# A fused attention and gated-MLP kernel: output tiles gated by their loads in the issue-order model, dummy matmuls up to the first scores, and another plan table

## The chip, the cores and the metric

The kernel runs on one core of one Trainium2 chip. The metric is device time in microseconds (us) of one execution; several executions are timed and the median is quoted with the range. Engines: PE is TensorE (PEld its weight loads), ACT is ScalarE, DVE is VectorE, POOL is GpSimd, SP is SyncE, which here only issues transfers (SPq is its queue). Every run of the changed kernel and of the experiments also reports the mean clock that the TensorE throttle granted; for the kernel before of the first rounds only the profiled execution has one.

## The reference

Two branches share one layer norm: an attention with 32 heads of 20 elements over 2,048 rows, and a gated MLP of 1,728 hidden units. The output is the input plus attention times the SiLU of the MLP.

```python
x = A_x                                   # 1 x 2048 x 640, bf16
xn = layernorm(x)
q, k, v = split(xn @ wqkv)                # 32 heads of 20
p = softmax(q @ k.T * 20 ** -0.5)
s = (p @ v) @ wo
h = sigmoid(xn @ w_gate) * (xn @ w_up)    # 2048 x 1728
g = silu(h @ w_down)
return x + s * g
```

## The kernel before

The scores are cut into 2,048 jobs of 128 x 512 (32 blocks, each of four heads and 512 rows). For most jobs ACT takes the exponential from PSUM; for the rest DVE approximates it (`iv`, then three passes `pb`). The three large engines work side by side for some 765 us, and the order in which each gets its instructions is found while the kernel is built: a time-stepped **order model** with fixed durations (`now`, `free[engine]`) hands out the next instruction to each engine. Its weights come from a **plan table** with one row of 18 numbers for each of the 32 blocks. No decision is taken on the chip: the model only fixes orders, and a wrong duration in it shows up as an engine standing at the head of its queue (in the profile of before DVE stands 1.08 us for a load, up to 695.40).

The parts that the change touches, with cuts:

```python
PLAN = (
    (0.25, 5, 0.15, 0.2, 0.5, 0, 0.4, 1, 0.0, 2, 2, 0, 0, 2, 4, 48, 1, 1),
    ...                                     # 32 rows
)
...
def dummies(n):                             # prologue; warm[0] is read by nobody
    for _ in range(n):
        nc.tensor.matmul(warm[0][:, 0:P], lhsT=ident, rhs=ident, start=True, stop=True)

def s_warm(eng):                            # first work of PE, at 2.5 us
    warm.append(psP.tile([P, 512], FP32, tag="pk", bufs=1, name="warm"))
    dummies(54)
...
def s_k(eng, c):                            # the four K matmuls of the first group
    pks[c] = psP.tile([P, 512], FP32, tag="pk", bufs=1, name="psk")
    k_mm(pks[c], 0, c)
def s_bound(eng):                           # the last PE work ahead of the first scores
    q_bound(pq[0], 0, pq[1])
...
def load_out(tt):                           # loads for one tile of 128 output rows
    ...
    nc.sync.dma_start(out=out_tiles[tt][0], in_=x2[tt * P:(tt + 1) * P, :])
    nc.sync.dma_start(out=out_tiles[tt][1], in_=gq_dram[tt * P:(tt + 1) * P, :])

def mk_out(tt, h, at):                      # half an output tile: 5 matmuls, one DVE pass, one addition
    def alloc():
        if h == 0:
            load_out(tt)
            if tt == 0:
                load_out(1)
        ...
    def ev():
        ... nc.vector.scalar_tensor_tensor(out=tmp, in0=st["ps"], scalar=0.25, in1=gqr[:, sl], ...)   # "otmp"
        add = nc.vector if h == 1 and claimed[0] == NJOB * NBLK else nc.gpsimd
        add.tensor_tensor(out=xr[:, sl], in0=tmp, in1=xr[:, sl], op=ALU.add)
        if h == 1:
            nc.sync.dma_start(out=out2[tt * P:(tt + 1) * P, :], in_=xr)
            if tt + 2 < TT - 4 and ...:
                load_out(tt + 2)
...
# end of a block: DVE copies the sums ("on<-bk"), they go to DRAM and come back as 128 x 16 ("lt<-ld")
free["DVE"] = now + T_ON
timed.append((free["DVE"] + 6.5, norm_pending[0]) + norm_a(norm_pending[0]))   # then DVE's reciprocal "rt<-lt"
```

Of the kernel before, what the change touches and what calls it, by code (L numbers as in the profile page):

```python
# [18 lines left out]
P = 128  # L19
# [19 lines left out]
            dmax=2, third=2, dord=0, mord=0, mfew=2, npv=4, held=48, burst=1, excl=1)  # L39
KEYS = tuple(RULE)  # L40
PLAN = (
    (0.25, 5, 0.15, 0.2, 0.5, 0, 0.4, 1, 0.0, 2, 2, 0, 0, 2, 4, 48, 1, 1),
    (0.25, 5, 0.15, 0.2, 0.5, 0, 0.4, 1, 0.0, 2, 1, 0, 3, 2, 4, 48, 1, 1),
    (0.25, 4, 0.15, 0.2, 0.8, 0.2, 0.4, 1, 8.0, 2, 2, 0, 0, 2, 4, 48, 1, 1),
    (0.25, 4, 0.15, 0, 0.8, 0.2, 0.4, 1, 0.0, 2, 2, 0, 0, 2, 4, 48, 0, 1),
    (0.25, 4, 0.15, 0, 0.8, 0.2, 0.4, 1, 0.0, 2, 2, 3, 0, 2, 4, 48, 0, 0),
    (0.2, 4, 0.15, 0.2, 0.2, 0.2, 0.4, 1, 0.0, 2, 2, 0, 0, 1, 4, 32, 1, 1),
    (0.25, 4, 0.15, 0.5, 0.8, 0.2, 0.4, 1, 0.0, 2, 2, 0, 0, 2, 4, 48, 1, 1),
    (0.25, 4, 0.3, 0.2, 0.35, 0.2, 0.4, 1, 0.0, 2, 2, 0, 0, 1, 4, 48, 1, 1),
    (0.25, 4, 0.3, 0.2, 0.35, 0.8, 0.4, 1, 0.0, 2, 2, 0, 0, 1, 4, 48, 1, 1),  # L50
    (0.3, 4, 0.3, 0.2, 0.35, 0.8, 0.4, 1, -2.0, 2, 2, 0, 0, 1, 4, 48, 1, 1),
    (0.3, 4, 0.3, 0.2, 0.35, 0.8, 0.4, 1, -2.0, 2, 2, 0, 0, 1, 4, 48, 1, 1),
    (0.25, 4, 0.15, 0.2, 0.2, 0.2, 0.4, 1, 0.0, 2, 2, 0, 0, 2, 4, 48, 0, 1),
    (0.2, 4, 0.15, 0.2, 0.2, 0.2, 0.2, 1, 0.0, 2, 2, 0, 0, 2, 4, 48, 0, 1),
    (0.25, 4, 0.15, 0.2, 0.2, 0.2, 0.4, 1, 0.0, 2, 0, 0, 0, 1, 4, 48, 0, 1),
    (0.25, 4, 0, 0.2, 0.2, 0.2, 0.4, 1, 0.0, 2, 0, 0, 0, 1, 4, 48, 1, 1),
    (0.25, 4, 0, 0, 0.2, 0.2, 0.4, 1, 4.0, 2, 0, 0, 0, 1, 4, 48, 1, 1),
    (0.3, 4, 0.15, 0.2, 0.2, 0.2, 0.4, 1, 0.0, 2, 2, 0, 0, 2, 4, 48, 1, 1),
    (0.3, 4, 0.15, 0.2, 0.2, 0.5, 0.7, 1, 0.0, 2, 2, 0, 0, 2, 4, 48, 1, 1),
    (0.25, 4, 0.15, 0.2, 0.2, 1.2, 0.4, 1, 0.0, 2, 2, 0, 0, 2, 4, 48, 1, 1),  # L60
    (0.25, 4, 0.15, 0.2, 0, 1.2, 0.4, 1, 0.0, 2, 2, 0, 0, 2, 4, 48, 1, 1),
    (0.25, 4, 0.3, 0.2, 0, 1.2, 0.4, 1, 0.0, 2, 2, 0, 0, 1, 4, 48, 1, 1),
    (0.25, 4, 0.3, 0.2, 0.5, 1.2, 0.4, 1, 0.0, 2, 1, 0, 0, 1, 4, 48, 1, 1),
    (0.25, 4, 0, 0.2, 0.8, 1.2, 0.4, 1, 0.0, 2, 2, 0, 0, 2, 4, 48, 1, 1),
    (0.25, 4, 0.15, 0.2, 0.2, 0.5, 0.4, 1, 0.0, 2, 1, 0, 0, 2, 4, 48, 1, 1),
    (0.45, 4, 0.15, 0.2, 0.2, 0.5, 0.4, 1, 0.0, 2, 1, 2, 0, 2, 4, 52, 1, 1),
    (0.25, 4, 0.15, 0.2, 0.2, 0.2, 0.4, 1, 0.0, 2, 1, 0, 0, 2, 4, 48, 1, 1),
    (0.25, 4, 0.15, 0.2, 0.2, 0.5, 0.4, 1, 0.0, 2, 1, 0, 0, 2, 4, 48, 1, 1),
    (0.25, 4, 0.15, 0.5, 0.2, 1.2, 0.4, 1, 0.0, 2, 2, 0, 2, 2, 4, 48, 1, 1),
    (0.25, 4, 0.15, 0.2, 0.35, 0.2, 0.4, 1, 0.0, 2, 2, 0, 0, 2, 4, 48, 1, 1),  # L70
    (0.25, 4, 0.15, 0.2, 0.2, 0.2, 0.4, 1, 0.0, 2, 0, 0, 0, 2, 4, 48, 1, 1),
    (0.25, 4, 0.15, 0.2, 0.35, 0.8, 0.4, 1, 14.0, 2, 1, 0, 0, 2, 4, 48, 1, 1),
    (0.25, 4, 0.15, 0.2, 0.2, 0.2, 0.4, 1, 0.0, 2, 2, 0, 0, 2, 4, 48, 1, 1),
)

PRO = (
# [35 lines left out]
def kernel(  # L112
# [146 lines left out]
    with tc.tile_pool(name="ln", bufs=2) as lp, \  # L259
# [105 lines left out]
        def s_k(eng, c):  # L365
            pks[c] = psP.tile([P, 512], FP32, tag="pk", bufs=1, name="psk")
            k_mm(pks[c], 0, c)

        def s_km(eng, c):
            maxed.append(c)  # L370
# [29 lines left out]

        def s_bound(eng):
            q_bound(pq[0], 0, pq[1])

        def s_qe0(eng):
            q_evac(pq[0], qts[0])
# [104 lines left out]
    def mk_k(g, c, at):  # L510
        st = {}

        def alloc():
            st["ps"] = misc_ps()
        mms = [lambda kd=kd: k_mm1(st["ps"], g, c, kd) for kd in range(KD)]
        return Item([("PE", alloc, [(T_MM, f) for f in mms]),
                     ("DVE", 0.66, lambda: k_evac(st["ps"], g, c), "free"),
                     ("DVE", 0.60, lambda: k_max(g, c), "", lambda t: mds_done(g, t))], at)

    def mds_done(g, t):  # L520
        if len(mk_n[g]) == NQC:
# [45 lines left out]
    def mk_ku(u, c, at):  # L567
        st = {}

        def alloc():  # L570
            st["ps"] = misc_ps()

        def ev():
            st["k"] = wk.tile([P, QC], BF16, tag="ku", bufs=2, name="ku")[0:UC, :]
            nc.vector.tensor_copy(out=st["k"], in_=st["ps"][0:UC, :])
            nc.sync.dma_start(out=kD[u][:, c * QC:(c + 1) * QC], in_=st["k"])

        def mx():
            if u not in mku:
                mku[u] = [wk.tile([UC, NQC], FP32, tag="mk4", bufs=2, name="mk4"), 0, None]  # L580
            nc.vector.tensor_reduce(out=mku[u][0][:, c:c + 1], in_=st["k"], axis=AXISX, op=ALU.max,
                                    apply_absolute_value=True)
            mku[u][1] += 1
            if mku[u][1] == NQC:
                mk = wk.tile([UC, 1], FP32, tag="mk", bufs=2, name="mk")
                nc.vector.tensor_reduce(out=mk, in_=mku[u][0], axis=AXISX, op=ALU.max)
                mku[u][2] = wk.tile([UC, UH], BF16, tag="mdu", bufs=2, name="mdu")
                nc.vector.tensor_scalar_mul(out=mku[u][2], in0=esum_u[0:UC, :], scalar1=mk[:, 0:1])

        def end(t):  # L590
            if mku[u][1] == NQC:
                ev_at[("mdu", u)] = t + 0.3
        return Item([("PE", alloc, [(T_MM, lambda kd=kd: u_mm(st, u, 1, c, kd)) for kd in range(KD)]),
                     ("DVE", 0.60, ev, "free", mark("kD", u, c)), ("DVE", 0.60, mx, "", end)], at,
                    pre=[("wu", u)])

    aqs = {}
# [180 lines left out]
    def load_out(tt):  # L778
# [3 lines left out]
        out_tiles[tt] = (o2[:, 0:D], o2[:, D:3 * D].bitcast(FP32))  # L782
        nc.sync.dma_start(out=out_tiles[tt][0], in_=x2[tt * P:(tt + 1) * P, :])
        nc.sync.dma_start(out=out_tiles[tt][1], in_=gq_dram[tt * P:(tt + 1) * P, :])

    def pool_hold(t):
        pool_from[0] = max(pool_at[0], t)
# [2 lines left out]
    def mk_out(tt, h, at):  # L790
        st = {}

        def alloc():
            if h == 0:
                load_out(tt)
                if tt == 0:
                    load_out(1)
            st["ps"] = misc_ps()

        def mm(kd):  # L800
# [4 lines left out]
        def ev():  # L805
# [7 lines left out]
            if h == 1:  # L813
                nc.sync.dma_start(out=out2[tt * P:(tt + 1) * P, :], in_=xr)
                if tt + 2 < TT - 4 and all(("d", (tt + 2) // 4, t4, i) in ev_at for t4 in range(4) for i in range(2)):
# [1 line left out]
        return Item([("PE", alloc, [(0.136, lambda kd=kd: mm(kd)) for kd in range(KD)]),  # L817
                     ("DVE", 0.40, ev, "free", lambda t: (mark("o", tt, h)(t), pool_hold(t)))], at, need=blk(NG - 1, tt // 4),
                    pre=[("d", tt // 4, t4, i) for t4 in range(4) for i in range(2)] + [("wo",), ("oc", tt // 4)] + (
                        [("o", tt - 2, 1)] if h == 0 and tt > 1 else []))  # L820


    wdf = wd.rearrange("p k e -> p (k e)")[:, 0:8 * D].bitcast(FP32)
# [290 lines left out]
    with tc.manual_schedule(engines={ENG.PE, ENG.Activation, ENG.DVE}):  # L1114
# [64 lines left out]
        while chain or items or glu_items or o_next < NQC or any(it.i < len(it.ops) for it in active):  # L1179
# [10 lines left out]
            if ("wo",) not in ev_at and base() >= PAIR and ("bD", NU - 1) in ev_at and all(  # L1190
                    v_at.get((NG // 2 - 1, t), 1e9) <= now for t in range(TT)) and all(
                    ev_at.get(("h", 2, kf), 1e9) <= now for kf in range(NFT)):
                ev_at[("wo",)] = now + 6.0
                for kd in range(KD):
                    nc.sync.dma_start(out=wo[kd], in_=A_wo[kd * P:(kd + 1) * P, :])
                for i in range(2):
# [35 lines left out]
            for eng in ("ACT", "DVE"):  # L1232
# [7 lines left out]
                    continue  # L1240
                if eng == "DVE" and norm_pending is not None and norm_pending[1] <= now and norm_pending[0] < NBLK - 1:
                    free["DVE"] = now + T_ON
                    timed.append((free["DVE"] + 6.5, norm_pending[0]) + norm_a(norm_pending[0]))
                    flex[pv_bank[0]] = now + T_ON + EL["DVE"]
                    pv_bank[0] = None
                    norm_pending = None
# [269 lines left out]
```

## Time and profile before

| | before |
|---|---|
| time | 811.13 us, 3 runs, 810.94 to 812.6 |
| profiled execution | span 811.3 us (time 813.0), mean granted clock 0.988 |
| busy share PE / DVE / ACT | 96% / 95% / 97% |
| first exponential to last | 29.88 to 795.51 us |
| from the last exponential to the end | 15.8 us |

The page gives the busy shares, the slices and the chain of waits; its own clock row already shows a dent in the second and in the tenth slice. The lines are in the prediction below, with their reading.

### The profile page before, as it was taken

What the parts mean: (1) busy time and instruction counts of PE and PEld (TensorE: products, weight loads), DVE (VectorE), ACT (ScalarE), POOL (GpSimd) and SP (SyncE); (2) the same over time, 40 slices, a digit from 0 to 9 for tenths busy, and PEclk for the clock granted to TensorE, in tenths of its full rate; (3) what the DMA queues carried; (4) which work ended last, traced back from release to release, by engine and by line L of the source; (5) the groups of instructions that cost most, each with busy time, mean ns of one, the idle gap of its engine ahead of it and who ended that gap; (6) DMA issues with size and microseconds to landing.
All of it is one profiled execution on the core that took longest, in us unless ns stands there. A gap on an engine that the chain in (4) does not pass through costs nothing.

```text
span 811.3 us, 17165 instructions
## 1 busy us (share of the span) xinstructions
PE 774.9 (96%) x6490; PEld 276.9 (34%) x6490; DVE 774.2 (95%) x1272; ACT 783.8 (97%) x1003; POOL 93.2 (11%) x107
## 2 busy tenths in 40 slices
PE   7899999999999999999999999999999999899995
PEld 6422233333333333333323323333332233233332
DVE  8799999998999999999999999999999999999996
ACT  8799999998999999999999999999999999999992
POOL 6000000000000000000000000000000001401346
PEclk9899999998999999999999999999999999999998
DMA  5511311122122222321113323143122331510431
GB/s 165 173 45 48 101 48 50 53 60 75 55 73 60 72 78 66 96 61 50 37 56 85 91 82 83 50 129 90 41 87 68 84 91 29 159 51 26 142 122 56
DMA packets 95876, 62.62 MB, mean 77 GB/s; under 512 B 36388, under 2 KB 89684, under 8 KB 95792
## 3 DMA queue, kind: packets, MB, share of 16 engines
q1 hardware_dynamic: 95504, 61.18, 26.9%
q8 instruction: 51, 0.84, 0.4%
q14 instruction: 33, 0.27, 0.1%
q10 hardware_dynamic: 288, 0.33, 0.1%
HBM read 47.84 MB, written 13.55 MB: 76 GB/s over the span
## 4 chain that ended last, share of the span: by engine, by line
ACT 55%; PE 28%; DVE 10%; issue 4%; DMA 2%; POOL 0%; SPq 0%; DVEq 0%; ACTq 0%; POOLq 0%
ACT pt L142 48%; PE scA L928 9%; PE bk L964 6%; PE bk L742 6%; DVE iv L1305 4%; PE bk L704 3%; ACT tnh L142 3%; DVE pb L1022 1%; PE bk L564 1%; ACT td L142 1%; DVE pb L1016 1%; DVE pb L1019 1%; PE bk L672 1%; ACT sq L338 1%; PE bk L802 1%
## 5 line engine op out<-in xcount | busy, mean ns | idle before, releaser
L142 ACT ACTIVATE pt<-scA 128x1024 bf16<-128x1024 f32 x696 | 715.0, 1235 | 2.7 <-PE bk L928 2.0
L1305 DVE TENSOR_SCALAR iv<-bk 128x512 int16<-128x512 f32 x497 | 330.5, 679 | 12.0 <-PE bk L928 10.5
L928 PE MATMUL scA<-q,kT 32*128 32x512 bf16 x1391 | 272.1, 384 | 15.7 <-ACT pt L142 11.6
L928 PE MATMUL bk<-q,kT 32*128 32x512 bf16 x657 | 206.6, 387 | 0.8 <-DVE otmp L809 0.5
L964 PE MATMUL bk<-pt,v 128*21 128x512 bf16 x1551 | 180.7, 382 | 0.0
L928 PEld LDWEIGHTS <-kT 32*128 32x128 bf16 x2048 | 86.7, 91 | 266.1 <-issue 253.7
L964 PE MATMUL bk<-pb,v 128*21 128x512 bf16 x994 | 155.8, 383 | 0.7 <-DVE pb L1016 0.5
L1022 DVE TENSOR_TENSOR pb<-iv,pb 128x2048 bf16<-128x2048 bf16 (+1 forms) x125 | 151.6, 1212 | 0.4
L704 PE MATMUL bk<-xnT,wgu 128*128 128x512 bf16 x520 | 144.3, 382 | 1.4 <-DVE iv L1305 0.6
L142 ACT ACTIVATE pt<-bk 128x512 bf16<-128x512 f32 x160 | 129.1, 807 | 4.3 <-PE bk L928 2.3
L1001 POOL TENSOR_TENSOR on_bf<-on,rl 128x512 bf16<-128x512 f32 x31 | 42.2, 1363 | 662.9 <-DVE rl L999 576.0
L1016 DVE TENSOR_SCALAR pb<-iv 128x2048 int16<-128x2048 int16 (+1 forms) x125 | 88.4, 707 | 0.7
L742 PE MATMUL bk<-wd,hT 128*128 128x320 bf16 x448 | 87.8, 307 | 1.2 <-DVE hT L724 1.0
L1019 DVE TENSOR_SCALAR pb<-iv 128x2048 int16<-128x2048 int16 (+1 forms) x125 | 85.9, 687 | 0.1
L964 PEld LDWEIGHTS <-v 128*21 128x21 bf16 x2545 | 47.5, 90 | 86.6 <-issue 70.2
L704 PEld LDWEIGHTS <-wgu 128*128 128x128 bf16 x520 | 39.0, 97 | 64.5 <-issue 41.7
L742 PEld LDWEIGHTS <-hT 128*128 128x128 bf16 x448 | 35.8, 98 | 43.9 <-issue 33.1
L142 ACT ACTIVATE tnh<-bk 128x512 bf16<-128x512 f32 (+1 forms) x56 | 45.9, 819 | 0.1
L564 PE MATMUL bk<-xnT,wu 128*128 128x512 bf16 x160 | 44.4, 382 | 0.0
L712 DVE SCALAR_TENSOR_TENSOR hT<-tnh,bk 128x512 bf16<-128x512 bf16 x52 | 35.4, 681 | 1.1 <-PE bk L704 0.5
L812 POOL TENSOR_TENSOR xnT<-otmp,xnT 128x320 bf16<-128x320 f32 x24 | 24.7, 1044 | 42.4 <-DVE otmp L809 30.6
L672 PE MATMUL bk<-wv,xnT 128*128 128x160 bf16 x280 | 28.2, 245 | 0.2
(116 smaller groups left out, 391.8 us busy)
## 6 DMA issues: line engine op xcount, KB each, us to landing
rl<-rd SPq DMA_DIRECT2D x124, 64.0 KB
wgu<-in_B_w_gate_dram SPq DMA_DIRECT2D x24, 320.0 KB
wgu<-in_B_w_up_dram SPq DMA_DIRECT2D x24, 320.0 KB
gq_dram<-gqs SPq DMA_DIRECT2D x24, 160.0 KB
xnT<-gq_dram SPq DMA_DIRECT2D x12, 320.0 KB
xt<-in_A_x_dram SPq DMA_DIRECT2D x16, 160.0 KB
oD<-on_bf SPq DMA_DIRECT2D x120, 20.0 KB
wd<-in_B_w_down_dram SPq DMA_DIRECT2D x1, 2080.0 KB
```

What stands on the lines that cost most here:

```text
L142: return nc.scalar.add_instruction(mybir.InstActivation(func=func, name=nc.get_next_instruction_name(), engine=ENG.Activation, ins=[nc.sca ...
L564: nc.tensor.matmul(st["ps"], lhsT=wus[u][:, kd, i, :], rhs=xnT[:, c, kd, :], start=(kd == 0), stop=(kd == KD - 1))
L672: nc.tensor.matmul(st["ps"][:, i * 2 * GC:(i + 1) * 2 * GC], lhsT=xn_tok(tts[i], kd), rhs=wvs[pr][:, kd, :], start=(kd == 0), stop=(kd == ...
L704: nc.tensor.matmul(st[key][0:fs, :], lhsT=w[:, i, kd, ko * P:ko * P + fs], rhs=xnT[:, c, kd, :], start=(kd == 0), stop=(kd == KD - 1))
L742: nc.tensor.matmul(st["ps"][:, 0:HD], lhsT=hT[0:fsz[kf], kf, t4 * P:(t4 + 1) * P], rhs=wd[0:fsz[kf], kf, h * HD:(h + 1) * HD], start=(kf = ...
L928: nc.tensor.matmul(dst, lhsT=kTs[gc(b)[0] % 2][32 * j:32 * j + 32, kt * P:(kt + 1) * P], rhs=qts[b % 3][32 * j:32 * j + 32, :], start=True ...
L964: nc.tensor.matmul(bank[pv_bank[0]][32 * j:32 * j + DH + 1, :], lhsT=lhsT, rhs=u["src"], start=first, stop=last, tile_position=(0, 32 * j) ...
L1001: nc.gpsimd.tensor_tensor(out=on_bf, in0=on, in1=rl, op=ALU.mult)
L1016: nc.vector.tensor_scalar(out=pb[:, 0, :, :].bitcast(I16), in0=iv, scalar1=0x7F80, scalar2=1, op0=ALU.bitwise_and, op1=ALU.bitwise_or)
L1019: nc.vector.tensor_scalar(out=pb[:, 1, :, :].bitcast(I16), in0=iv, scalar1=0x007F, scalar2=0x3F00, op0=ALU.bitwise_and, op1=ALU.bitwise_or)
L1022: nc.vector.tensor_tensor(out=pb[:, 1, :, :], in0=iv.bitcast(BF16), in1=pb[:, 1, :, :], op=ALU.mult)
L1305: nc.vector.tensor_scalar(out=d["iv"][:, j, :], in0=bank[bk], scalar1=B_OFF, scalar2=0.0, op0=ALU.add, op1=ALU.max)
```

## The change

The intent: (1) let the order model know when the loads of an output tile land, so that DVE is not sent to a tile whose data is not there; (2) keep PE busy before the first scores, so that its clock is not halved there (0.50 from 27.81 to 34.64 us in the profile of before); (3) a plan table found anew (another seed of the search) for the changed model. Two durations are also made truer: DVE's last maximum of a group takes 1.05 instead of 0.60 us, and the reciprocal comes 7.0 instead of 6.5 us after the copy of the sums.

```diff
 PLAN = (
-    (0.25, 5, 0.15, 0.2, 0.5, 0, 0.4, 1, 0.0, 2, 2, 0, 0, 2, 4, 48, 1, 1),
+    (0.25, 4, 0.3, 0.2, 0.2, 0.2, 0.4, 1, 0.0, 2, 0, 0, 2, 2, 4, 48, 1, 1),
 ...                                  all 32 rows
         def s_k(eng, c):
             ...
             k_mm(pks[c], 0, c)
+            if len(pks) == NQC:
+                warm[0] = psP.tile([P, 2 * P], FP32, tag="tp", bufs=4, name="warm2")
+                dummies(14)
 ...
             q_bound(pq[0], 0, pq[1])
+            dummies(10)
 ...
-                     ("DVE", 0.60, lambda: k_max(g, c), "", lambda t: mds_done(g, t))], at)
+                     ("DVE", 1.05 if c == NQC - 1 else 0.60, lambda: k_max(g, c), "", lambda t: mds_done(g, t))], at)
 ...
         nc.sync.dma_start(out=out_tiles[tt][1], in_=gq_dram[tt * P:(tt + 1) * P, :])
+        ev_at[("ol", tt)] = now + 4.0
 ...
                 load_out(tt)
-                if tt == 0:
-                    load_out(1)
 ...
-                        [("o", tt - 2, 1)] if h == 0 and tt > 1 else []))
+                        [("o", tt - 2, 1)] if h == 0 and tt > 1 else []), gates={1: [("ol", tt)]})
 ...
                 ev_at[("wo",)] = now + 6.0
+                load_out(0)
+                load_out(1)
 ...
-                    timed.append((free["DVE"] + 6.5, norm_pending[0]) + norm_a(norm_pending[0]))
+                    timed.append((free["DVE"] + 7.0, norm_pending[0]) + norm_a(norm_pending[0]))
```

## The prediction

> **What bounds the kernel now.** I read the page first (busy shares, slices, the chain that ended last), then the engines' busy times by stretch, then the timeline of the worst stretches, since the page alone says only that everything is full.
>
> ```profile
> span 811.3 us, 17165 instructions
> PE 774.9 (96%) x6490; PEld 276.9 (34%) x6490; DVE 774.2 (95%) x1272; ACT 783.8 (97%) x1003; POOL 93.2 (11%) x107
> ...
> PEclk9899999998999999999999999999999999999998
> ...
> ACT 55%; PE 28%; DVE 10%; issue 4%; DMA 2%; POOL 0%; SPq 0%; DVEq 0%; ACTq 0%; POOLq 0%
> ...
> L142 ACT ACTIVATE pt<-scA 128x1024 bf16<-128x1024 f32 x696 | 715.0, 1235 | 2.7 <-PE bk L928 2.0
> L1305 DVE TENSOR_SCALAR iv<-bk 128x512 int16<-128x512 f32 x497 | 330.5, 679 | 12.0 <-PE bk L928 10.5
> L928 PE MATMUL scA<-q,kT 32*128 32x512 bf16 x1391 | 272.1, 384 | 15.7 <-ACT pt L142 11.6
> ```
>
> Three engines are 95 to 97% busy. The 2,048 score jobs are split: ACT takes the exponential of most of them, DVE approximates it for 497. ACT leads the chain with 55%, and its exponentials (L142) waited only 2.7 us in all, so ACT sets the pace; what is left to win is its idle time and its share of jobs. To find the idle time I cut the span into stretches (columns: length, then PE, PEld, DVE, ACT, POOL busy with counts, granted clock, DMA share, GB/s).
>
> ```profile
> 24.40:27.81 3.41, 1.41 (x8) 0.55 (x6) 2.14 (x6) 1.36 (x3) 0.00 (x0) 1.00 0.00 0
> 27.81:34.64 6.83, 5.95 (x40) 3.78 (x41) 3.91 (x6) 4.20 (x7) 0.00 (x0) 0.50 0.80 228
> 184.82:188.24 3.42, 2.03 (x13) 0.52 (x12) 3.39 (x7) 3.37 (x5) 0.00 (x0) 1.00 0.27 72
> 188.24:195.07 6.83, 6.42 (x31) 2.36 (x30) 5.76 (x10) 5.14 (x7) 0.00 (x0) 0.50 0.51 132
> 707.03:710.44 3.41, 1.90 (x16) 0.84 (x13) 3.32 (x6) 3.36 (x5) 0.00 (x0) 1.00 0.94 276
> 28.00:36.00 8.00, 7.12 (x55) 4.57 (x54) 4.51 (x7) 5.08 (x8) 0.00 (x0) 0.59 0.86 257
> 184.00:200.00 16.00, 14.15 (x109) 4.63 (x105) 13.63 (x22) 13.90 (x17) 0.00 (x0) 0.79 0.33 84
> 692.00:708.00 16.00, 14.33 (x138) 4.28 (x136) 14.18 (x23) 14.55 (x18) 7.40 (x6) 1.00 0.48 138
> ```
>
> Twice the TensorE clock falls to 0.50 for 6.83 us, each time after 3.41 us in which PE was busy only 41% and 59%. ACT loses 8.00 - 5.08 = 2.92 us around the first (1.88 of it before the first exponential at 29.88), 16 - 13.90 = 2.10 us around the second, and 1.45 us in 692 to 708, where the output projection starts and the clock is full. The timeline tells that third loss (start, length, instruction; in brackets the idle time and what ended it):
>
> ```profile
> 695.40 0.49 DVE L809 SCALAR_TENSOR_TENSOR otmp<-bk,xnT 128x320 f32<-128x320 f32 x1 [1.08 <-DMA xnT<-gq_dram]
> ...
> 695.95 0.37 PE L928 MATMUL bk<-q,kT 32*128 32x512 bf16 x1 [0.53 <-DVE otmp L809]
> ...
> 696.36 0.60 ACT L142 ACTIVATE pt<-bk 128x512 bf16<-128x512 f32 x1 [0.51 <-PE bk L928]
> ```
>
> DVE stands 1.08 us at the head of its queue for a load of the output stage, the PE waits for the bank, ACT for the score: one late transfer reaches all three.
>
> [...] the two drops are at 27.81 and 188.24, 160.43 us or 47.0 windows apart, and each lasts two windows. [...] here windows with 41% and 59% recorded activity were enough, while 56% at 707 was not punished. [...] Here an output store issued at 692.77 let the load into its buffer go at 696.14, 3.37 us later, so the 4.0 us that the change writes into its model is of the right size.
>
> **The change part by part.** I compared the issue orders of both kernels.
>
> *Dummies.* 24 more 128-column matmuls, 14 after the last K matmul of the prologue and 10 after the bound matmul. The warm ones of the prologue take 0.33 us for three, end to end; with the drain of about 0.22 us shown by one, each adds some 0.055. So 14 take 0.77 us and lie inside the 1.17 us idle before the bound matmul (27.74, waiting for DVE's md); 10 take 0.55 us plus drain, inside the bound's wait plus q's evacuation of 0.69 us. Neither is on the path. They raise the 24.40 window from 1.41 to about 2.2 of 3.41 us, 64%, and the gap before the first scores (0.79 us) nearly closes. [...] Worth: the bound matmul falls from 572 to 386 ns, 0.19 us; ACT's 2.92 - 1.88 = 1.04 us of idle mostly goes. I book 1.0 us.
>
> *Gates.* The order model now lets DVE take an output tile 4 us after its load was issued. No instruction disappears. Both first tile loads were already issued at 539 in the trace, so hoisting them buys nothing; the gate matters for tiles 2 and up. Of the 1.45 us I book 1.0.
>
> *Plan table.* All 32 rows differ, so the whole order from the first scores on is another one. The counts hardly move: exponentials on ACT 160 + 2 x 695 + 1 = 1551 become 158 + 2 x 693 + 5 = 1549, DVE's jobs 497 become 499. A job costs ACT about 0.46 us (start to start, two-job exponentials run at 0.93): 0.9 us less, minus two more groups at some 0.05: 0.8 us. DVE gains two jobs of 0.679 + (702 + 690 + 1219)/4 ns = 1.33 us each, 2.7 us, against more than 20 us that it was idle: hidden. The old order's hole at 185 to 188 is not there any more: three score fills in succession had 0.54, 0, 0 us of other matmul work between them, 1.3 us of PE work against 3.2 us of ACT work. Removing it is worth the 2.10 us, I book 2.0. But the new order has one such place too, at fill 682 of 698 (about 775 us): 0.24, 0, 0 us between three fills, 1.0 us of PE work against 3.5 of ACT work, just before the third group of output tiles, which waits for its normalised input. That is emptier than the old hole. [...] A drop costs about what the old one did, so -1.0 on average.
>
> *Small ones.* DVE's longer last maximum (1.05 instead of 0.60) and 0.5 us more before a reciprocal only make the model truer; the reciprocal waited 1.7 us in all. I book nothing.
>
> Sum: 1.0 + 1.0 + 0.8 + 2.0 - 1.0 = 3.8 us off 811.1, which is 807.3.
>
> **The rivals.** (1) *The clock stays half in the prologue*: [...] 64% is only just above the 59% that fell. Then 1.0 us is lost: 808.3. (2) *A new hole replaces the old*: the drop near 775 comes in every run and, so late, has no slack behind it: 809 or a little more. For it speaks the count above, against it the 56% at 707 that went unpunished. (3) *ACT stays full and all is won*: ACT's idle in the exponential stage is 1.04 + 4.7 us (the second summed over 36 to 797 us); all of it with 0.8 and 0.2 gives 804.4, the floor unless the 14 us after the last exponential shrink, and nothing in the change touches those. (4) *The new order has late transfers elsewhere*, or POOL's additions hold up DVE (in 692 to 708 POOL is busy 7.40 us and one DVE pass L1016 took 1.76 us instead of 0.70): some 2 us, giving 809.5; possible, since output tiles now come in single matmuls between other work.
>
> **Range and chances.** The centre is 807.3; 804.5 is the floor of rival 3, 810.3 is rivals 2 and 4 in part together. A change of 2% would be 16 us; all the idle time of ACT is under 6, so faster or slower by that much has a chance of 1% each.
>
> **What would show each step.** Dummies right: granted clock 1.00 in 28 to 36 and ACT busy about 6 of those 8 us. Plan right: no half clock at 185 to 195, ACT's idle over 36 to 797 below 3 us. Gates right: DVE's wait at the output tiles for the gq load below 0.5 us in all (2.0 now). Rival 2: clock 0.50 for 6.83 us from about 775 to 785, possibly only in some runs, whose times would then differ by about 2 us. Wrong altogether if the time stays above 811 or falls below 804: then a drop elsewhere, or work after the last exponential, would be what I failed to see.

The last term, -1.0, is half of the 2.0 booked for the old hole, and the half was the author's estimate. The 4.0 us of the gate stand on the 3.37 us alone. A "window" here and below is a stretch of 3.41 us, half the length of the two drops in the profile of before, which begin 160.43 us or 47 such stretches apart; what sets their place, and on what the clock is decided, was not shown.

## The result, and the profile after

| | before | after |
|---|---|---|
| time, 4 runs each on one chip | 811.04 us (810.15 to 812.6) | 809.54 us (809.04 to 811.45) |
| ratio, 95% interval | | 0.9984 (0.9961 to 1.0006) |
| mean clock of the profiled run | 0.988 | 0.996 |

Ratios here are the mean time of one kernel's runs over that of the other's runs of the same rounds, so not quite the ratio of the medians quoted. The result is correct. ACT's idle time between the first and the last exponential fell from 5.2 us to 2.3 in the profiled pair; the stretch behind the last exponential grew from 15.8 us to 17.3.

The page of the changed kernel, the rows that answer to those of before:

```profile
span 807.7 us, 17151 instructions
...
PE 766.2 (95%) x6464; PEld 277.9 (34%) x6516; DVE 773.5 (96%) x1274; ACT 781.8 (97%) x1003; POOL 87.4 (11%) x107
...
PEclk9999999999999999999999999999999999999998
...
L142 ACT ACTIVATE pt<-scA 128x1024 bf16<-128x1024 f32 x698 | 712.1, 1224 | 1.8 <-PE bk L931 1.5
```

The profiled pair went from 811.3 to 807.7 us, almost the forecast 3.8. But the medians of four runs moved by only 1.5. Where that profile was taken, the clock row has no dent left: no window at half clock from the start to the end of the exponentials. The busy times by stretch, for the three stretches where the kernel before lost time (columns as in the prediction):

```profile
28.00:36.00 8.00, 7.42 (x75) 4.42 (x77) 6.91 (x12) 6.46 (x8) 0.00 (x0) 1.00 0.82 242
184.00:200.00 16.00, 14.51 (x140) 4.96 (x141) 15.66 (x26) 15.95 (x20) 0.00 (x0) 1.00 0.22 61
692.00:708.00 16.00, 13.99 (x105) 5.65 (x97) 13.22 (x23) 15.06 (x19) 5.10 (x6) 1.00 0.43 129
```

ACT's busy time in the first two is 6.46 (was 5.08) and 15.95 us (was 13.90), both at full clock. The third is less good than hoped: 15.06 of 16 us against 14.55. The timeline of the changed kernel shows why (start, length, engine, instruction; in brackets the idle time before it and what ended it):

```profile
702.14 1.27 SPq L817 DMA_DIRECT2D out_dram<-xnT  x1
...
703.50 0.89 SPq L788 DMA_DIRECT2D xnT<-gq_dram  x2
...
706.69 0.89 DVE L812 SCALAR_TENSOR_TENSOR otmp<-bk,xnT 128x320 f32<-128x320 f32 x2 [2.29 <-DMA xnT<-gq_dram]
707.23 0.37 PE L931 MATMUL bk<-q,kT 32*128 32x512 bf16 x1 [1.56 <-DVE otmp L812]
...
708.57 0.60 ACT L142 ACTIVATE pt<-bk 128x512 bf16<-128x512 f32 x1 [1.51 <-PE bk L931]
```

It is the same chain as before (DVE at the head of its queue for `gq`, PE behind it, ACT behind that), now in one piece of 2.29 us instead of three that summed to 2.0. The DVE pass that frees the buffer ended at 700.27, and the model counts 4.0 us from there. On the chip the load stood in SP's queue behind the store of tile 1, which waits for POOL's additions (1.0 us); SP then needed 1.27 us to issue that store where other issues take 0.35. So the load went out 3.2 us after the buffer was free and landed another 3.2 us later.

### The profile page after: what moved, and what is told of

Same layout as the page of the kernel before. It is cut to its first block, busy times and chain, and to the rows that moved or that the text cites. A ratio compares the mean times of both kernels' runs of the same rounds, so it can differ in the third digit from the quotient of the medians.

```text
span 807.7 us, 17151 instructions
## 1 busy us (share of the span) xinstructions
PE 766.2 (95%) x6464; PEld 277.9 (34%) x6516; DVE 773.5 (96%) x1274; ACT 781.8 (97%) x1003; POOL 87.4 (11%) x107
## 4 chain that ended last, share of the span: by engine, by line
ACT 55%; PE 25%; DVE 11%; issue 5%; DMA 2%; SPq 1%; POOL 1%; ACTq 0%; DVEq 0%; POOLq 0%
ACT pt L142 51%; PE scA L931 8%; PE bk L708 6%; PE bk L967 4%; PE bk L746 4%; DVE iv L1310 4%; ACT tnh L142 2%; DVE pb L1025 1%; ACT td L142 1%; PE bk L676 1%; DVE pb L1022 1%; POOL xnT L815 1%; DVE pb L1019 1%; SPq L264 1%; PE bk L838 1%
## 5 line engine op out<-in xcount | busy, mean ns | idle before, releaser
L931 PE MATMUL scA<-q,kT 32*128 32x512 bf16 x1391 | 271.3, 382 | 16.9 <-ACT pt L142 12.6
L931 PE MATMUL bk<-q,kT 32*128 32x512 bf16 x657 | 199.7, 383 | 1.8 <-DVE otmp L812 1.6
L967 PE MATMUL bk<-pt,v 128*21 128x512 bf16 x1549 | 182.6, 382 | 0.0
L931 PEld LDWEIGHTS <-kT 32*128 32x128 bf16 x2048 | 88.1, 90 | 262.2 <-issue 249.0
L708 PE MATMUL bk<-xnT,wgu 128*128 128x512 bf16 x488 | 138.4, 382 | 2.3 <-issue 1.3
L142 ACT ACTIVATE pt<-bk 128x512 bf16<-128x512 f32 x158 | 125.2, 792 | 2.0 <-PE bk L931 1.9
L1004 POOL TENSOR_TENSOR on_bf<-on,rl 128x512 bf16<-128x512 f32 x31 | 40.4, 1303 | 646.4 <-DVE rl L1002 556.9
L746 PE MATMUL bk<-wd,hT 128*128 128x320 bf16 x448 | 85.0, 302 | 1.2 <-DVE iv L1310 0.5
L815 POOL TENSOR_TENSOR xnT<-otmp,xnT 128x320 bf16<-128x320 f32 x24 | 21.2, 897 | 57.7 <-DVE otmp L812 45.1
```

What stands on the lines that cost most here:

```text
L142: return nc.scalar.add_instruction(mybir.InstActivation(func=func, name=nc.get_next_instruction_name(), engine=ENG.Activation, ins=[nc.sca ...
L708: nc.tensor.matmul(st[key][0:fs, :], lhsT=w[:, i, kd, ko * P:ko * P + fs], rhs=xnT[:, c, kd, :], start=(kd == 0), stop=(kd == KD - 1))
L746: nc.tensor.matmul(st["ps"][:, 0:HD], lhsT=hT[0:fsz[kf], kf, t4 * P:(t4 + 1) * P], rhs=wd[0:fsz[kf], kf, h * HD:(h + 1) * HD], start=(kf = ...
L931: nc.tensor.matmul(dst, lhsT=kTs[gc(b)[0] % 2][32 * j:32 * j + 32, kt * P:(kt + 1) * P], rhs=qts[b % 3][32 * j:32 * j + 32, :], start=True ...
L967: nc.tensor.matmul(bank[pv_bank[0]][32 * j:32 * j + DH + 1, :], lhsT=lhsT, rhs=u["src"], start=first, stop=last, tile_position=(0, 32 * j) ...
L1004: nc.gpsimd.tensor_tensor(out=on_bf, in0=on, in1=rl, op=ALU.mult)
```

## The experiments

Three theories were put to the test. **A** (the prediction's): the parts act each for itself, and their gains add up. **B** (luck of the clock): much of the difference of the profiled pair is the number of half-clock windows that each execution happened to draw. **C** (formed after the second set): the dummies cost time, not by running, but because their 48 PE instructions (24 matmuls, 24 weight loads) move every later fetch of PE's instruction stream (the packets of set 3, one of them at 329.28 instead of 333.32 us). All kernels were correct. (The letters in the expectations of before_again and after_again mean something else: A there is that the drop at 188 comes in some runs only, B that it comes in every run.) Runs of one set share a chip and the runs of the kernel before. Source lines shift by a few between the kernels; L928, L931 and L934 are the same score matmul.

| run | change against | median us (range) | kernel before, same rounds | ratio (95%) | mean clock |
|---|---|---|---|---|---|
| before_again | nothing | 810.18 (808.85 to 811.06) | 810.37 | 0.9990 (0.9973 to 1.0008) | 0.9935 |
| dummies_only | before + dummies | 812.41 (811.6 to 815.68) | 810.37 | 1.0027 (1.0006 to 1.0049) | 0.9943 |
| after_no_dummies | after - dummies | 809.30 (807.0 to 811.68) | 810.37 | 0.9982 (0.9962 to 1.0003) | 0.9932 |
| after_again | nothing | 809.97 (808.57 to 811.66) | 810.37 | 0.9991 (0.9973 to 1.0009) | 0.9953 |
| plan_only | before + plan | 823.79 (823.59 to 824.56) | 811.33 | 1.0151 (1.0124 to 1.0178) | 0.9880 |
| gates_only | before + gates | 831.29 (830.81 to 832.19) | 811.33 | 1.0243 (1.0215 to 1.0270) | 0.9852 |
| gq_first | after, load moved | 811.09 (808.84 to 813.07) | 811.33 | 0.9990 (0.9963 to 1.0017) | 0.9933 |
| gq_first_nd | same, no dummies | 809.66 (808.54 to 809.85) | 811.33 | 0.9972 (0.9951 to 0.9994) | 0.9938 |
| before_tiny24 | before + 48 instructions | 812.72 (810.83 to 814.54) | 811.25 | 1.0015 (0.9994 to 1.0036) | 0.9928 |
| dummies_warm42 | dummies_only - 24 instructions | 812.69 (811.15 to 815.26) | 811.25 | 1.0018 (0.9996 to 1.0041) | 0.9917 |
| after_nd_tiny24 | after_no_dummies + 48 instructions | 812.18 (809.64 to 813.23) | 811.25 | 1.0005 (0.9984 to 1.0025) | 0.9912 |
| gq_first_nd_tiny48 | gq_first_nd + 96 instructions | 810.30 (809.66 to 811.08) | 811.25 | 0.9984 (0.9966 to 1.0002) | 0.9938 |
| after_wide30 | after - 48 instructions | **808.50** (807.08 to 809.42) | 811.49 | **0.9961** (0.9945 to 0.9976) | 0.9957 |
| before_wide30 | dummies_only - 48 instructions | 811.32 (809.5 to 813.14) | 811.49 | 1.0001 (0.9983 to 1.0018) | 0.9928 |
| after_third | nothing | 810.06 (809.51 to 811.87) | 811.49 | 0.9988 (0.9972 to 1.0005) | 0.9942 |

(Six runs each, four of plan_only and gates_only; the mean clock is that of the same runs. With a line drawn at 2%, only gates_only is slower and every other run is the same as the kernel before.)

### Set 1: how much is luck, and what do the dummies do alone?

`before_again` and `after_again` are the two kernels unchanged. `dummies_only` is the kernel before with this and nothing else; `after_no_dummies` is the changed kernel without it:

```diff
             k_mm(pks[c], 0, c)
+            if len(pks) == NQC:
+                warm[0] = psP.tile([P, 2 * P], FP32, tag="tp", bufs=4, name="warm2")
+                dummies(14)
 ...
             q_bound(pq[0], 0, pq[1])
+            dummies(10)
```

> The kernel before, unchanged, to see each run's mean granted clock. One clock drop of 6.83 us at half rate takes 6.83 x 0.5 / 811 = 0.0042 off the mean clock; the profiled run of before had 0.988 (drops at 28 and 188 us), the profiled run of the changed kernel 0.996 (no drop). Theory A [...]: the runs split, most at 0.992 (prologue drop alone) and 809.5 to 811.2 us, some at 0.988 and about 2 us longer. Rival B (the drop at 188 is part of the schedule): nearly all runs at 0.988, all within 0.5 us of each other. Ratio to before 1.000 either way.

> The changed kernel, unchanged, on the same chip as the three others. Theory A: clock 0.996 in most runs and 809.0 to 809.8 us, a drop (0.992) in one run of three to five with about 2 us more; ratio to before 0.997 to 0.9985. Rival B (before always has its drop at 188): ratio near 0.9955, 3.6 us, as the two profiles differ.

> The kernel before plus the 24 dummy matmuls alone; the order of everything else is that of before. Theory (the dummies keep the clock up in the prologue and ACT keeps what it gains): granted clock 1.00 in 28 to 36 us, ACT idle after its first exponential near 0 there instead of 1.04 us, 1.0 to 1.2 us faster than before (ratio 0.9985 to 0.9988). Rival (slack later takes the gain back): same clock in the prologue, but the time within 0.3 us of before. As the order of the middle is that of before, the drop at 188 should again come in some runs only.

> The changed kernel without its 24 dummy matmuls (plan and gates stay). Theory: half clock from about 28 us for 6.83 us again, 1.0 to 1.2 us slower than the changed kernel, so about equal to before (ratio 0.999 to 1.001). Rival (slack takes it back): the time of the changed kernel, ratio 0.998.

**Measured.** The same kernel before, profiled once more, spans 808.8 us instead of 811.3. Its stretches (the first is the 3.41 us window that ends 47 windows before the drop at 188.27):

```profile
24.43:27.84 3.41, 1.62 (x12) 0.68 (x9) 2.27 (x7) 1.35 (x3) 0.00 (x0) 1.00 0.00 0
...
28.00:36.00 8.00, 6.86 (x65) 3.85 (x66) 6.05 (x11) 6.54 (x10) 0.00 (x0) 1.00 0.79 234
184.00:200.00 16.00, 14.15 (x133) 4.29 (x131) 14.82 (x25) 15.08 (x18) 1.27 (x1) 0.89 0.27 73
```

PE was busy 47% of the window at 24.43 and the clock stayed at 1.00; in the first profile the same window at 41% was followed by two windows at 0.50. After the hole at 188 there is a drop again, but of one window (0.89 over 16 us) instead of two. An execution is otherwise reproduced to about 0.2 us: the copies of the sums at the block ends of after, after_again and after_no_dummies lie within 0.2 us of each other up to block 22. So **B holds in part**: the clock differs from run to run (0.989 to 0.996 for the kernel before in these rounds), and the base profile, at 0.988, was a slow draw. The drop at 188 itself is no luck, only its length is (see the count below).

Two expectations of this set missed. after_again lay a little above its 809.0 to 809.8 us. after_no_dummies was expected 1.0 to 1.2 us slower than the changed kernel and was 0.7 us faster in the medians; its profile shows no half clock at 28 us.

To take the luck out, all 134 runs of all sets were put on straight lines of time against mean clock, one common slope, one level for each kernel. The slope is 0.514 +- 0.027 us for each 0.001 of clock. One 3.41 us window at half clock is 0.0021 of the mean, so it costs **1.08 us**. The levels at equal clock are used below; the fit gives each an error of 0.1 to 0.4 us. That leaves out differences between the sets, which ran on different chips: the kernel before alone lies at 809.3, 810.1, 809.9 and 809.9 us in the four. With a term for each set, the differences taken below keep their sign and change by up to 0.6 us.

| at clock 0.995 | us | | at clock 0.995 | us |
|---|---|---|---|---|
| before (50 runs) | 809.8 | | after (16 runs) | 810.1 |
| dummies_only | 812.4 | | after_no_dummies | 808.4 |
| before_tiny24 | 811.8 | | after_nd_tiny24 | 810.0 |
| before_wide30 | 810.4 | | after_wide30 | 808.7 |
| dummies_warm42 | 811.1 | | gq_first, gq_first_nd, gq_first_nd_tiny48 | 810.3, 808.9, 809.7 |

The unexpected result is dummies_only: with the orders of the kernel before on every engine, it takes 2.6 us more at equal clock. Most of it lies in one place: the copies of the sums lie 0.3 us behind those of the repeated kernel before up to block 11, and 1.8 us behind at block 12. DVE's reciprocal waits longer for the sums to come back, first the repeated kernel before, then dummies_only:

```profile
326.67 0.44 SPq L982 DMA_DIRECT2D lt<-ld  x1
...
329.56 0.25 DVE L988 RECIPROCAL rt<-lt 128x16 f32<-128x16 f32 x1 [0.98 <-DMA lt<-ld]
```

```profile
326.99 0.44 SPq L986 DMA_DIRECT2D lt<-ld  x1
...
331.38 0.25 DVE L992 RECIPROCAL rt<-lt 128x16 f32<-128x16 f32 x1 [2.53 <-DMA lt<-ld]
```

From issue to use the 8 KB take 4.4 us instead of 2.9, with the same transfers issued around them. That nothing in the program explains this was left open until set 3.

### Set 2: do the parts add up, and is the wait at 706 the place in the queue?

`plan_only` is the kernel before with the new table alone; `gates_only` the kernel before with everything but table and dummies.

> The kernel before with the new plan table alone: no dummies, no gates, the old durations in the order model. Theory of the prediction (the parts add up): the hole at 185 us goes, so about 2 us faster than the kernel before in runs where that hole drew a drop, so 808.5 to 810.5. Rival (a table is the result of a search against one order model, and is worth nothing with another): the kernel's own order model, read out while it builds, ends at 769.6 with this pair, against 757.7 for the kernel before and 758.7 for the changed one; then the time is about 12 us longer, 820 to 824, with ACT and PE waiting in the last blocks for the output stage.

> The kernel before with the gates, the hoisted first loads and the changed durations of the order model, but with the old plan table and no dummies. Theory of the prediction (the parts add up): ACT's idle time of 1.45 us where the output stage starts mostly goes, 1.0 us faster, 809.5 to 810.5. Rival (the table belongs to the model it was searched with): the order model ends at 767.2 with this pair, 9.5 later than the kernel before, so 819 to 822 us.

**Measured.** 12.5 and 20.0 us slower than the kernel before of the same rounds (medians). **Theory A falls**: neither the table nor the gates are worth anything without the other. plan_only is through with its exponentials at 793.0 us, as early as the kernel before (795.5 and 792.7 in its two profiles), and then needs 28.9 us to the end instead of 15.8: output tiles are left over. Its last two stretches, the second from the end of the exponentials:

```profile
760.00:800.00 40.00, 38.69 (x362) 16.16 (x360) 33.76 (x55) 34.52 (x49) 4.33 (x4) 1.00 0.16 39
793.00:822.00 29.00, 18.22 (x127) 11.39 (x124) 17.36 (x33) 2.39 (x6) 13.80 (x16) 0.89 0.26 80
```

ACT, the bound until then, is busy 2.39 of the last 29 us. The kernel's own order model had told it: it ended at 769.6 and 767.2 for the mixed pairs, against 757.7 for the kernel before and 758.7 for the changed one. It foretold the sign and most of plan_only's loss, and half of gates_only's.

`gq_first` is the changed kernel with the load of `gq` for tile tt + 2 moved ahead of the store of tile tt; the orders of the four computing engines stay. `gq_first_nd` is the same without dummies.

```diff
             if h == 1:
-                nc.sync.dma_start(out=out2[tt * P:(tt + 1) * P, :], in_=xr)
-                if tt + 2 < TT - 4 and all(...):
-                    load_out(tt + 2)
+                nxt_ok = tt + 2 < TT - 4 and all(...)
+                if nxt_ok:
+                    load_out(tt + 2, part=1)        # gq alone
+                nc.sync.dma_start(out=out2[tt * P:(tt + 1) * P, :], in_=xr)
+                if nxt_ok:
+                    load_out(tt + 2, part=2)        # x, into the buffer that the store reads
```

> The changed kernel, with one thing moved: the load of gq for output tile t+2 is issued ahead of the store of output tile t instead of behind it (the load of x stays behind it, since it goes into the buffer the store reads). The order on PE, ACT, DVE and POOL stays what it was. Theory (the gate counts the landing from the last reader of the buffer, but the load stands in the queue behind a store that waits for POOL): DVE's wait of 2.29 us for gq at about 706.7 falls below 0.8 us, ACT's idle time over 690 to 720 falls from 1.8 to below 0.8 us, block 28's copy comes 1.0 to 1.5 us earlier than 722.63, and the time falls by about 1 us against the changed kernel. Rival (the load is slow because the transfer engines are busy, share 0.91 in 704 to 708): gq lands at about 706 as before, DVE still waits over 1.5 us, and the time stays within 0.4 us of the changed kernel's. Second rival (slack): the wait at 706 goes, but the time stays, because something behind it, such as the last blocks' output tiles or the tail, takes it back.

> The same move of the gq load, and the 24 dummy matmuls taken out: the candidate to beat both kernels. If the gain at 706 is real and the dummies are worth nothing or cost a little, this is the fastest: 807.5 to 808.5 as a median, 2 us or more below the kernel before. If the dummies are worth a drop of the clock in most runs, it is slower than gq_first by about 1 us, and more of its runs show a mean clock of 0.992 or less.

**Measured.** A miss: gq_first wins nothing, and DVE waits 2.34 us as before.

```profile
702.08 1.45 SPq L788 DMA_DIRECT2D xnT<-gq_dram  x1
...
703.62 0.38 SPq L822 DMA_DIRECT2D out_dram<-xnT  x1
...
706.65 0.89 DVE L814 SCALAR_TENSOR_TENSOR otmp<-bk,xnT 128x320 f32<-128x320 f32 x2 [2.34 <-DMA xnT<-gq_dram]
```

The load is now first, but the slow issue stayed where it was, at 702, and hit the load instead of the store. Its turn in the queue was not the whole cause: at 702 SP was slow with the store (1.27 us) and slow with the load (1.45). In gq_first_nd no issue at 702 is slow, one at 707.8 is, and DVE waits 0.98 us; its median of 809.66 missed the 807.5 to 808.5 expected. So the stall goes with the dummies, though SP's queue holds the same instructions with and without them.

### Set 3: the instruction fetch

The trace records the transfers of an instruction queue, q8. On the page of the changed kernel it has this row (packets, MB, share of the 16 engines):

```profile
q8 instruction: 51, 0.84, 0.4%
```

51 packets of 16 KB, one for each 256 of the instructions in PE's queue: 13,070 / 256 = 51.1, counted in after_again, since the trace of the changed kernel lacks 52 matmul records. Each packet takes 0.88 to 1.41 us (median 1.02). Their times fit the stalls: in the changed kernel packets start at 142.54 and 701.88, and SP's slow issues at 142.53 and 702.14; in after_no_dummies packets at 421.51 and 750.44, slow issues at 421.62 and 750.43. These are not picked cases: in the 17 profiles together, behind the first 40 us, 145 issues of SP took over 0.9 us (up to 1.84; the median issue takes 0.34), and 142 of them overlap one of these packets in time; by chance it would be about one in seven (an estimate from 49 packets of 1.0 us and issues of 1.2 us in 768 us). The reverse does not hold, since most packets that meet an issue leave it as short as ever. In dummies_only one falls at 329.28, between issue and landing of the late sums; in before_again its counterpart comes at 333.32. The dummies' 48 instructions are 0.19 of the 256 that go with one packet, on average 3 us earlier at a packet every 15.9 us.

How a packet of 1 us holds up a whole transfer is not shown: the times agree (packet at 329.28, the 8 KB used 4.4 instead of 2.9 us after their issue), but which of the 16 engines carried what was not looked at.

`before_tiny24` adds 48 PE instructions to the kernel before where PE is idle anyway (0.78 us up to 8.76 in the profile of before), 20 us ahead of the scores. `after_nd_tiny24` does the same to after_no_dummies, and `gq_first_nd_tiny48` to gq_first_nd with 48 matmuls. `dummies_warm42` keeps the dummies and takes 12 of the 54 warm matmuls away.

```diff
             dummies(54)
+            for _ in range(24):
+                nc.tensor.matmul(warm[0][0:1, 0:1], lhsT=ident[:, 0:1], rhs=ident[:, 0:1], start=True, stop=True)
```

```diff
-            dummies(54)                       # dummies_warm42, on top of dummies_only
+            dummies(42)
```

> The kernel before, with 24 matmuls of one column (48 PE instructions with their weight loads) added right behind the 54 warm matmuls at the start, where PE stands idle for 0.78 us at 8 us; no dummy near the scores, every other order unchanged. Theory (the dummies cost time because they move the fetches of PE's instruction stream: the traces show a 16 KB packet of the instruction queue for every 256 PE instructions, each holding a transfer engine for about 1.1 us): from 31 us on the fetches fall where they fell with the 24 dummies alone, at about 329.3 instead of 333.3, in the middle of the load of the 128x16 sums (issued 327); that load lands 4.3 instead of 2.6 us after its issue, DVE's reciprocal waits about 2.5 us instead of 1.0, block 12's copy comes 1.5 us later after block 11's than in the kernel before, and the time is 811.8 to 813 in median, 1.5 to 2 above the kernel before's. Rival (the dummies themselves, between the K matmul and the scores, cost time): nothing changes here, the reciprocal waits 1.0, and the time is the kernel before's within 0.5 us.

> The kernel before with the 24 dummies near the scores, and 12 of the 54 warm matmuls at the start taken out, so that 24 PE instructions fewer stand ahead of everything and each later fetch comes about 2 us later than with the dummies alone. Theory (fetches): the fetch that fell at 329.3 falls at about 331.3, after the sums have landed; the reciprocal at about 330 waits 1.0 us, and the time is 810.4 or a little less in median, 2 us below the 812.4 of the dummies alone. Rival (the dummies themselves): the time stays at 812 or more. [...]

> The changed kernel without its 24 dummies, with 24 matmuls of one column at 8 us instead, so PE's fetches fall as in the changed kernel. Theory (fetches): a fetch falls at about 701.8, an issue of the output store at 702.1 takes 1.3 us instead of 0.35, gq lands as late as in the changed kernel and DVE waits about 2.3 us for it; the time is the changed kernel's, 809.5 to 810.5. Rival (the dummies themselves): DVE's wait is 1.0 us or less longer than without dummies and the time is that of the changed kernel without dummies, 808.5 to 809.3.

> The fastest so far (the gq load issued ahead of the store, no dummies), with 48 matmuls of one column at the start, so that the fetch at 707.4 and those around it come about 8 us earlier, at 697 to 699, ahead of the gq load (issued 703). Theory (fetches): no issue in 702 to 708 takes over 1 us, DVE's wait for gq is at most the 0.98 us of that kernel, and the time is its 809.7 less 0 to 1 us, unless the 48 matmuls push the first transposes back by more than the idle 0.78 us. Rival: the wait is the time that the load needs beside the other transfers (share 0.88 in 704 to 708), and nothing is won; a fetch that falls on another load costs 1 us elsewhere.

**Measured.** before_tiny24 has no dummy near the scores, and its reciprocal waits like that of dummies_only:

```profile
328.00 0.44 SPq L984 DMA_DIRECT2D lt<-ld  x1
...
332.24 0.25 DVE L990 RECIPROCAL rt<-lt 128x16 f32<-128x16 f32 x1 [2.35 <-DMA lt<-ld]
```

The packet came at 330.16, and the kernel is 2.0 us above the kernel before at equal clock (1.5 in the medians). In after_nd_tiny24 the packet is back at 702.36, the store's issue at 702.33 takes 1.36 us, DVE waits 2.2 us, and it is 1.6 us above after_no_dummies at equal clock. **Theory C holds: the loss comes back without any dummy near the scores, as soon as the packets fall in the same places. The rival, that the dummies cost by being there, is not needed for it** (what may be left of it is in set 4). Three misses belong here. The median of after_nd_tiny24, 812.18, lies above the 809.5 to 810.5 expected, at a clock of 0.9912. dummies_warm42 did what was expected in the trace (packet at 330.97, wait 1.10 us, 1.3 us below dummies_only at equal clock), but its median did not come down, because its six runs had a clock of 0.9917; whether the missing warm matmuls have a part in that is open (its profile shows no half clock before 187 us). And gq_first_nd_tiny48, without a packet between 701.4 and 716, still waits 1.0 us for `gq`: that much comes without a packet, as the rival had it, which put it on the other transfers (not shown apart). It is 0.9 us above gq_first_nd at equal clock; its block copies fall behind by 0.4 us by block 9 and another 0.5 by block 21, where its packets fall otherwise, but what was hit there was not followed up.

### Set 4: the dummies without their instructions

The cause was still open in one point: could the clock's gain be had without the fetch's cost? `after_wide30` and `before_wide30` keep all 24 dummies, but make 48 of the 54 warm matmuls into 24 of double width. The columns are the same, the count of PE instructions is that of the kernel without dummies.

```diff
-            dummies(54)
+            for _ in range(24):
+                nc.tensor.matmul(warm[0][:, 0:2 * P].rearrange("p (a c) -> p a c", a=2), lhsT=ident,
+                                 rhs=ident.rearrange("p (a c) -> p a c", a=1).broadcast_to((P, 2, P)), start=True, stop=True)
+            dummies(6)
```

> The changed kernel with all its 24 dummies, but the 54 warm matmuls at the start made 24 of double width and 6 single, the same columns in 24 fewer matmuls, so that 48 PE instructions less stand ahead and every later fetch falls where it falls without dummies. Theory (the dummies cost by their instructions alone, and gain by the clock): the fetch near 702 falls at about 707, no issue of the output store at 702 takes over 1 us, DVE's wait for gq is 1.5 us or less instead of 2.3; the mean clock over six runs is 0.994 to 0.996 as with dummies; the time is 808.0 to 809.0 in median, 1 to 1.8 us below the changed kernel's and 2 to 3 us below the kernel before's. Rival (the dummies cost by being there): the time is the changed kernel's within 0.5 us although the fetches have moved.

> The kernel before with the 24 dummies near the scores and the same shortening of the warm matmuls, so that its PE instruction count is that of the kernel before. Theory: the fetch that fell at 329.3 falls at 333 again, the reciprocal at about 330 waits 1.0 us, block 12's copy comes 24.0 us after block 11's (25.6 with the dummies alone), and the time is 2 us below the 812.4 of the dummies alone: 809.5 to 810.8, at or up to 1 us below the kernel before's of the same rounds, by the drops of the clock that the dummies save. Rival: it stays at 812 or more.

> The changed kernel once more, as the yardstick of these rounds. Expected 809.5 to 810.5, mean clock 0.995, the fetch at about 701.9, DVE's wait for gq 2.3 us.

**Measured.** after_wide30 is the fastest kernel: 808.50 us, 0.9961 of the kernel before, and 1.6 us below the changed kernel in the same rounds. Its timeline at the place of the wait:

```profile
702.48 0.37 SPq L820 DMA_DIRECT2D out_dram<-xnT  x1
...
702.94 0.89 SPq L791 DMA_DIRECT2D xnT<-gq_dram  x2
...
705.91 0.89 DVE L815 SCALAR_TENSOR_TENSOR otmp<-bk,xnT 128x320 f32<-128x320 f32 x2 [1.19 <-DMA xnT<-gq_dram]
706.46 0.37 PE L934 MATMUL bk<-q,kT 32*128 32x512 bf16 x1 [0.46 <-DVE otmp L815]
...
707.80 0.60 ACT L142 ACTIVATE pt<-bk 128x512 bf16<-128x512 f32 x1 [0.41 <-PE bk L934]
```

Against the same lines of the changed kernel above: the store's issue takes 0.37 instead of 1.27 us (the packet comes at 706.32), DVE waits 1.19 instead of 2.29, ACT 0.41 instead of 1.51. The block copies say the same: up to block 27 those of after_wide30 lie 0.33 us behind those of the changed kernel's profile, at block 28, behind this place, they are 0.96 us ahead; a half-clock window at 772 then took that back in this one execution. before_wide30 confirms the other half: the packet is at 335.12, the reciprocal waits 1.15 us, and at equal clock it is 2.0 us below dummies_only. It stays 0.7 us above the kernel before, about twice the error, so some cost of the dummies themselves is not excluded in the old order. Its median, 811.32, missed the expectation by 0.5 us at a clock of 0.9928; its profiled run had three half-clock windows behind the hole at 188. after_third repeats the changed kernel: 810.06, wait 2.1 us, packet at 702.02.

**Which dents does the clock get?** Each of the 17 profiles shows where it was halved, so they can be counted:

| place | orders of before, and the two mixed pairs | orders of after |
|---|---|---|
| ahead of the first scores, no dummies | before, before_tiny24, plan_only, gates_only yes; before_again no | gq_first_nd, gq_first_nd_tiny48 yes; after_no_dummies, after_nd_tiny24 no |
| the same, with dummies | 0 of 3 | 0 of 5 |
| hole at 188 | 6 of 6 with table and model of before, 1 to 3 windows, 1.5 on average | 0 of 9 |
| hole at 772 | 0 of 6 | 6 of 9, one window each |
| 706 to 708, start of the output stage | 2 of 6 (before_again, dummies_warm42), one window each | 2 of 9 (after_again, gq_first), one window each |

(The two mixed pairs count in the first line alone. Single windows elsewhere: one in after_no_dummies at 588, two in before_tiny24 at 9 and 334, and five in the mixed pairs, plan_only's double one at 208 counted as one.) The prediction took the 56% at 707 for unpunished; in before_again the window there, also at 56%, was followed by half clock.

The line for 772 is the new hole of the plan table, here in after_wide30, the window of the hole and the one behind it:

```profile
768.10:771.51 3.41, 1.91 (x14) 0.68 (x13) 3.41 (x7) 3.41 (x6) 0.00 (x0) 1.00 0.14 41
771.51:774.92 3.41, 3.31 (x14) 1.56 (x13) 2.07 (x3) 2.87 (x5) 0.58 (x1) 0.50 0.00 0
```

PE at 56% in one window, half clock in the next, and ACT at 2.87 of 3.41 us.

## Why the prediction was right or wrong

Over all runs the changed kernel averages 810.1 us at clock 0.9949 (16 runs), the kernel before 811.25 at 0.9921 (50 runs): 1.1 us, 1.5 in the medians of the first rounds, against 3.8 forecast. The forecast of a gain was right in sign; most of its size did not come.

- **What bounds the kernel**: right inside the exponential stage. ACT leads with 97% before and after, and the waits followed there reach it. (The 4.7 us of idle time that the prediction sums for ACT behind 36 us reads 4.2 us up to the last exponential; nothing rests on the difference.)
- **Dummies, the clock**: right, and of about the right size. No halving ahead of the scores in 8 profiles with them, 6 in 9 without. Over all runs in the new order the mean clock is 0.9947 with dummies (28 runs) and 0.9930 without (24): 0.0017 x 514 = 0.9 us, with an error of 0.3; 1.0 was booked. Single pairs scatter: gq_first, with dummies, has 0.9933, gq_first_nd 0.9938.
- **Dummies, their cost: this step failed.** "Neither is on the path" was argued from the matmuls' own time, and of that it is true: at equal clock after_wide30 is 0.3 us above after_no_dummies, within the error. But their 48 instructions moved the fetches, one of which, at 701.88, fell on SP's issue at 702.14. That cost 1.4 us (after against after_wide30 at equal clock) to 1.6 us (after_nd_tiny24 against after_no_dummies; 1.1 with a term for each set), at least as much as the clock gave. The prediction had no term for it.
- **Gates: booked 1.0, and no such term exists.** Gates and table can't be parted: alone they cost 20.0 and 12.5 us. In 692 to 708 ACT gained 0.5 us, and the waits for `gq` went from 2.0 to 2.3 us. "The 4.0 us that the change writes into its model is of the right size" compared 3.37 us from the issue of a store to the load behind it; the model counts from the last reader of the buffer, and from there to the landing it took 6.4 us.
- **Plan table, the holes**: right. The old hole cost a halving in 6 of 6 profiles and is gone; the new one costs a window in 6 of 9, near the half that the forecast assumed. That half was the author's estimate, and PE's busy share alone does not give it: windows with PE 53 to 70% busy were followed by the halving here, one with 47% (before_again, 24.43) was not. Net 1.5 - 0.67 = 0.8 windows, 0.9 us; 2.0 - 1.0 was booked.
- **The base**: I took the two drops of one profile, four half-clock windows and 0.988, for the normal case. The mean of 50 runs is 0.9921, two windows fewer. Altogether the clock gave 0.0028 x 514 = 1.4 us where 1.0 + 2.0 - 1.0 = 2.0 were booked.
- **Jobs and "nothing in the change touches" the tail**: the share of jobs was booked at 0.8 us. Tables, gates, jobs and durations together, at equal clock and with the old fetches, gave 809.8 - 808.4 = 1.4 us (1.0 with a term for each set), where 1.8 were booked. The tail was a miss inside that: from the last exponential to the end the new order takes 16.8 to 17.3 us in all nine profiles, the old one 15.8 to 16.2 in all six.
- **The small ones**, of which nothing was booked: with the later reciprocal in the model and the new orders its waits went from 1.7 us to none; the two were not parted.
- **Rivals**: the second (a new hole) came true in six of nine profiles; the fourth (late transfers elsewhere, some 2 us, 809.5) came nearest, for a reason that it did not name. The third, all is won, came true in no run: even in the profiled one, without a halving, ACT kept 2.3 us of idle time and the tail grew.

The sums: forecast 2.0 from the clock and 1.8 from the rest. Measured 1.4 from the clock, and 0.3 lost by the rest: 1.4 from table, gates and durations, less 1.4 to 1.6 for the moved fetches; what remains is within the error of the levels. That 1.4 from the clock comes near the 2.0 booked is partly luck, since base, hole and dummies were each off. Open are why one packet of 1.0 us delays the sums by 1.5 us, and which feature of a window, if not PE's busy share, makes the clock fall.

## What to carry to other kernels

One profile is one draw (0.988 in the one used here, 0.9921 over 50 runs): before a gain is booked from the dents of a profile's clock row, compare that run's clock and time with the other runs. Instructions that fit into idle time were not free here: 48 of them moved the fetches of PE's stream by some 3 us, and with them which transfer was late, for 1.4 us; making other matmuls wider restored the count (after_wide30). A table that comes from a search can be worth nothing in another model than its own (12.5 us lost here), and a gate in such a model should count stores that stand in front in the queue, here 6.4 us to the landing instead of 4.0; that such a gate would gain time was not tried.

## What the runs showed of the fetch and the clock

- The fetch: one packet for each 256 PE instructions (51 packets for 13,070 entries, after_again). What it costs PE itself was not looked at, but it costs others: each 16 KB packet takes 0.88 to 1.41 us, an issue of SP beside it can take 0.9 to 1.8 us instead of 0.34, an 8 KB load is used 4.4 instead of 2.9 us after its issue, and moving the packets was worth 1.4 to 2.0 us of 810.
- The clock: windows with PE 41%, 56%, 59% and even 70% busy (gq_first, 769.77) were followed by half clock, and others with 45% (24.69 in after_no_dummies) and 47% (24.43 in before_again) were not. What tells them apart was not found. A halving lasted one, two or three windows (3.41, 6.83, 10.24 us).
- The price of a half-clock window in this kernel, which ACT bounds: 1.08 us (by the slope over 134 runs), of the 1.7 us that PE loses (half of 3.41).
